# An expert layer whose row loads go four per unit, and a late row fetch that moves to one queue

## The chip, the cores and the metric

The kernel runs on one core of a Trainium2 chip. Its engines are TensorE (PE, matrix products; PEld is its weight load), VectorE (DVE), ScalarE (ACT), GpSimd (POOL) and SyncE (SP, which issues transfers). The metric is the device time in microseconds of one execution, lower is better.

## The reference, cut to what matters

```python
x = attention(q, k, v)                       # 4608 tokens of 512, linear attention with decay
logits = x @ w_gate                          # 8 experts
expert_idx = argmax(logits, axis=1)
gate_w = softmax(logits)[arange(N), expert_idx]
for e in range(8):                           # each token goes to one expert
    mask = expert_idx == e
    h = maximum(x[mask] @ w1[e], 0.0)        # 512 -> 1024
    out[mask] = gate_w[mask, None] * (h @ w2[e])   # 1024 -> 512
h = maximum(out @ w_in, 0.0)                 # the dense layer, 512 -> 2048
return (h * h) @ w_out                       # 2048 -> 512
```

## The kernel before

The kernel has three parts, and each begins before the one ahead of it has ended. The first, to about 185 us, computes attention and leaves the tokens as rows in DRAM (`x_d`) with their logits (`l_d`), and sorts the tokens by expert: `qidx` and `gidx` hold, for each expert, up to 640 rows in five tiles of 128.

The second is the expert layer, about 185 to 750 us. It is a loop over 64 units `u`, eight for each expert `e` (`f` is the unit within it). A unit holds 128 of the 1024 hidden features. In TensorE's order iteration `u` computes the first product of unit `u + 1` (`first`, lines 806 to 808, 24 matmuls on two halves of 320 tokens) and the second product of unit `u` (`second`, lines 830 to 832, 15 matmuls). Every product is split in a high and a low part, so there are three matmuls where one would do. Between the two products ScalarE takes the positive part of a half into `hh` (line 812) and VectorE the remainder into `hl` (line 813). The buffer of `hh` and `hl` has six places; the second product of the last six units is done at the end.

While expert `e` runs, the rows of expert `e + 1` are fetched. In the iteration with `f == 0`, `gather(e + 1)` puts 20 indirect loads on POOL's queue (line 270, tile `xs`: five tiles of 128 rows, each in four quarters of 512 bytes a row), and with `f == 1` five loads of the logits of those rows follow (tile `glg`). An indirect load is an instruction of POOL, and POOL takes its instructions in order. Two units after its own number (three for the rows of expert 1) a tile is turned by VectorE (`transp`, line 778). When an expert's last unit is done, `finish` scales its five accumulators on ScalarE (line 841) and POOL writes them to their rows of `y_d` (line 291). These writes stand ahead of the next expert's loads on POOL. The gate of an expert is computed at its unit 5 from the logits that came in.

Beside this SyncE loads the experts' weights (line 107), and VectorE and ScalarE prepare the weights of the dense layer, a job in nearly each unit.

The third part is the dense layer, in five steps of row tiles. It needs rows of `y_d` of all experts. While the last expert's five tiles are finished one after the other, SyncE fetches the first row tiles (`fetch`, line 709, four parts each, tile `yi`), VectorE turns them (line 722), sums and splits them (lines 734 and 747), and the first products of the dense layer (line 1146) follow. A fetch of rows waits for the writes of `y_d` issued so far. The tile numbered 3 is fetched in the last turn of that loop; behind it SyncE issues two loads of weight tiles (`stream`, line 319, 1 MB each).

Of the kernel before, what the change touches and what calls it, by code (L numbers as in the profile page):

```python
# [7 lines left out]
F32 = mybir.dt.float32  # L8
# [5 lines left out]
ALU = mybir.AluOpType  # L14
# [8 lines left out]
CT = CAP // 128  # L23
# [4 lines left out]
LEAD = 2  # L28
# [21 lines left out]
def body(ctx, tc, att, tab_v, tab_x, masks, wg, ident, pick, cst, wu, wd, out):  # L50
    nc = tc.nc
    vec, act, pe, pool, sp = nc.vector, nc.scalar, nc.tensor, nc.gpsimd, nc.sync

    def scope(stack, name, bufs, space=None, side=None, reuse=None):
        kw = {"space": space, "side": side, "reuse_waits": reuse}
        kw = {k: v for k, v in kw.items() if v is not None}
        return stack.enter_context(tc.tile_pool(name=name, bufs=bufs, **kw))

    const = scope(ctx, "const", 1)
    xs_p = scope(ctx, "xs_p", 1)  # L60
# [11 lines left out]
    x_d = dram.tile([NTOK, 512], F32, name="x_d")  # L72
# [10 lines left out]
    gidx = places.tile([128, NS], I32, name="gidx")  # L83
# [10 lines left out]
    qidx = places.tile([128, 4, NS], I32, name="qidx")  # L94
# [10 lines left out]
    def load_unit(u, on=None):  # L105
        raw = on.tile([128, CT, 4, 128], F32, tag="xs", name="raw").rearrange("p a b c -> p (a b c)")[:, 0:1024] if on else pools["stg"].tile([128, 1024], F32, tag="raw", name="raw")
        sp.dma_start(out=raw, in_=wu[u])
        return raw
# [18 lines left out]
    def load_wide(v, s):  # L127
        raw = pools["cr_p"].tile([128, 512, 2], I32, tag="craw", name="craw")
        sp.dma_start(
            out=raw.rearrange("p n t -> p (n t)"), in_=wd[v, :, 512 * s:512 * s + 512].bitcast(I32)  # L130
        )
        return raw
# [124 lines left out]
    def indices(rt, n, inv, gi, si, gf=None):  # L257
        f = rt.tile([128, n], F32, tag="f", name="f")
        vec.scalar_tensor_tensor(
            out=f, in0=inv[:, n:2 * n], scalar=128.0, in1=inv[:, 0:n], op0=ALU.mult, op1=ALU.add  # L260
        )
        for o in (gi, gf):
            if o is not None:
                vec.tensor_scalar(out=o, in0=f, scalar1=-1.0, scalar2=0.0, op0=ALU.add, op1=ALU.max)
        g = rt.tile([128, n], F32, tag="g", name="g")
        vec.tensor_scalar(out=g, in0=inv[:, 0:n], scalar1=0.0, scalar2=FAR, op0=ALU.is_equal, op1=ALU.mult)
        vec.scalar_tensor_tensor(out=si, in0=f, scalar=-1.0, in1=g, op0=ALU.add, op1=ALU.add)

    def fetch_rows(xs, src, index):
        pool.indirect_dma_start(  # L270
            out=xs, out_offset=None, in_=src, in_offset=bass.IndirectOffsetOnAxis(ap=index, axis=0),
        )
# [8 lines left out]
    x_q = x_d.rearrange("n (a c) -> (n a) c", a=4)  # L281
# [46 lines left out]
    with ExitStack() as es:  # L328
# [307 lines left out]
        for t in range(NT):  # L636
# [3 lines left out]
            if t in (1, 2, 4):  # L640
                c = {1: 2, 2: 3, 4: 4}[t]
# [53 lines left out]
    yi = {}  # L695

    def columns():
        return [xt_p.tile([128, 4, CAP], F32R, tag=f"xt{s}", name=f"xt{s}") for s in range(2)]


    def rows_of(t):

        return y_d[128 * t:128 * t + 128, :].rearrange("(t i) (a c) -> a i t c", i=32, a=4)
# [3 lines left out]
    def fetch(dst, t, known=True, on=None, parts=range(4)):  # L707
        for a in parts:
            d = (on or sp).dma_start(out=dst[32 * a:32 * a + 32], in_=rows_of(t)[a])
            if not known:  # L710
                for p in sent:
                    tc.add_manual_dep(
                        d.ins, p.name,
                        mybir.DependencyInfo(mybir.DependencyClass.Sync, mybir.DependencyReason.DATA),
                        reason="the rows come from all of them",
                    )
                if len(yi) < 2:
                    read.append(d.ins)
# [32 lines left out]
    with ExitStack() as es:  # L751
# [3 lines left out]
        acc_a = scope(es, "acc_a", 1, PSUM, reuse="tile")  # L755
        xs_t, xt_t, lg_t, h_t, acc, gate = {}, {}, {}, {}, {}, {}

        def gather(e):
            xt_t[e] = columns()
            xs = xs_p.tile([128, CT, 4, 128], F32, tag="xs", name="xs")  # L760
            for i in range(0 if e else LEAD, CT):
                j = CT * e + i
                if e == 0:
                    fetch_rows(xs[:, i].rearrange("p q c -> p (q c)"), x_d[:, :], gidx[:, j:j + 1])
                    continue
                for q in range(4):
                    fetch_rows(xs[:, i, q], x_q, qidx[:, q, j:j + 1])
            xs_t[e] = xs

        def transp(e, i):  # L770
            xs = xs_t[e]
# [158 lines left out]
        tiles = range(LEAD)  # L930
# [18 lines left out]
        ends.pop(0)()  # L949
        steps[4]()  # L950
        indices(rt, NS, inv, gidx, sidx, gidf)
        gather(0)
        for f in ends:
            f()
        top = rt.tile([128, 1], F32, tag="top", name="top")
# [17 lines left out]
        sm = scope(es, "sm", 2, reuse="tile")  # L973
# [37 lines left out]
        for u in range(NU):  # L1011
            e, f = divmod(u, 8)
            v = u + AHEAD + 1
            if v < NU:
                raw[v] = load_unit(v)
            if u + 1 in work:
                what, j, r = work[u + 1]
                if what != "sum":
                    wide.append(load_wide(2 * j + r, 0 if what == "in" else 1))
            v = u + AHEAD  # L1020
            job, rests = None, []
            if last_job:
                f_ = next(last_job)
                if f_:
                    f_()
                last_job = None
            if v in raw:
                rests.append(split_unit(v, raw.pop(v), vec))
            if u in work:
                what, j, r = work[u]  # L1030
                if what == "in":
                    job = narrow(wide.pop(0), ("ca", "cb")[r], made)
                elif what == "sum":
                    job = left_factors(j, *made[2 * j:], r)
                else:
                    job = split_wide(2 * j + r, wide.pop(0))
            if v == NU + 2:
                assert not last_job and not wide
                early.close()
                w_d = scope(late_es, "w_d", 4, side="right", reuse="tile")  # L1040
                x0_p = scope(late_es, "x0_p", 1, side="right", reuse="tile")
            if v in (NU, NU + 1):
                stream(w_a, 4 + v - NU)
            if v >= NU + 2:
                stream(w_d, v - NU - 2)
            if e + 1 < NE:
                if f == 0:
                    gather(e + 1)
                if f == 1:
                    lg_t[e + 1] = fetch_logits(sm, gidx[:, CT * (e + 1):CT * (e + 2)], CT)  # L1050
            if e + 1 < NE:
                turns = {3: [0], 4: [1], 5: [2], 6: [3, 4]} if e == 0 else {i + 2: [i] for i in range(CT)}
                rests += [transp(e + 1, i) for i in turns.get(f, [])]
            for f_ in rests[:1]:
                f_()
            if job:
                next(job)
            for f_ in rests[1:]:
                f_()
            if u == NU - 3:  # L1060
                with tc.block():
                    tc.mark_branch_hint_location("rest", "LikelyTaken", [mybir.EngineType.PE])
            if u + 1 < NU:
                first(u + 1, (1,) if u + 1 < MORE else (0, 1))
            if f == 5:
                gate[e] = gate_of(sm, lg_t.pop(e), CT)
            if job:
                next(job)
                last_job = job
            if u < NU - FIN:  # L1070
                second(u, range(LEAD if u < MORE else 0, CT))
                if f == 7:
                    finish(e)
        rest_of()
        for i in range(CT):
            for u in range(NU - FIN, NU):
                second(u, [i])
            if i == CT - 1:
                turn(yi[0][:, 3], x0_t[0][:, 1], None)
                low = first_row(1, 4, 2)  # L1080
                fetch(yi[0][:, 2], 3, False, sp, (0, 1))
                fetch(yi[0][:, 2], 3, False, pool, (2, 3))
                for f in low:
                    f()
                for _ in range(2):
                    stream(w_a)
            finish(NE - 1, [i])
            if i < 2:
                if i == 0:
                    yi[0] = xs_p.tile([128, CT, 4, 128], F32, tag="xs", name="yi")  # L1090
                fetch(yi[0][:, 2 + i], i, False)
            if i == 2:
                fetch(yi[0][:, 4], 2, False)
            if i == 3:
                first_factors()
                turn(yi[0][:, 2], x0_t[0][:, 0], None)
                for f in first_row(0, 4, 2):
                    f()
# [383 lines left out]
```

## Time and profile before

| what | value |
|---|---|
| runs | 1487.53, 1497.63, 1511.9 us; median 1497.63 |
| profiled execution | 1501.78 us, its span 1500.0 us |
| TensorE busy | 1387.7 us, 93% of the span |
| VectorE, ScalarE, POOL busy | 832.5, 547.7, 357.4 us |
| mean granted clock of TensorE | 0.954 |

Busy time of an engine is the time in which its instructions ran; matmuls are pipelined, so a busy TensorE is not one at its peak. [...] In the rows below a bracket gives the idle time of the engine just before the instruction, and what ended it; "issue" means that the profile shows nothing that was waited for, "remote" that the signal's origin was not found.

### The profile page before, as it was taken

The numbers are of one execution on the slowest core, as the hardware profiler recorded it, in microseconds if no ns is written. First come the engines' busy times: TensorE is split into PE (matmuls) and PEld (weight loads), VectorE is DVE, ScalarE is ACT, GpSimd is POOL, SyncE is SP. The second block draws the span as 40 slices with busy tenths as digits, with TensorE's granted clock in tenths as the row PEclk, the third lists the DMA queues.
The fourth block names the chain that finished last, engine by engine and source line by source line (L and its number), as shares of the span: only waits on it lengthen the run. The fifth ranks groups of instructions, "written<-read, shape, count | busy, mean of one in ns | idle before, by whom it ended". The sixth has DMA issues, their size and how long they took to land. (4 is left out here: it accounts for less than half of the span.)

```text
span 1500.0 us, 21528 instructions
## 1 busy us (share of the span) xinstructions
PE 1387.7 (93%) x8121; PEld 1174.6 (78%) x8121; DVE 832.5 (56%) x1512; ACT 547.7 (37%) x1064; POOL 357.4 (24%) x368
## 2 busy tenths in 40 slices
PE   8989998596959897989989999999999999999998
PEld 6877797394939685969888888888888888888887
DVE  5767766383838584866368646524563456435422
ACT  1222333251515252434245444424442344334421
POOL 2232275425160716261122101200030002100000
PEclk9999998696969997989999999999999999999999
DMA  9999745262636554554768566665666566665563
GB/s 317 317 281 290 217 156 170 84 225 86 234 97 208 187 190 153 191 168 165 258 215 299 206 212 231 226 222 201 220 225 222 208 218 234 217 217 196 196 225 113
DMA packets 107488, 311.02 MB, mean 207 GB/s; under 512 B 20430, under 2 KB 55502, under 8 KB 85360
## 3 DMA queue, kind: packets, MB, share of 16 engines
q1 hardware_dynamic: 97440, 288.28, 56.4%
q0 software_dynamic: 9936, 21.28, 4.7%
q8 instruction: 66, 1.08, 0.3%
q14 instruction: 46, 0.38, 0.1%
HBM read 257.98 MB, written 52.58 MB: 207 GB/s over the span
## 5 line engine op out<-in xcount | busy, mean ns | idle before, releaser
L1146 PE MATMUL b<-xt,wq 128*128 128x512 f32 (+1 forms) x1296 | 266.8, 364 | 6.3 <-ACT xt L743 5.3
L1146 PEld LDWEIGHTS b<-xt,wq 128*128 128x128 f32 x1296 | 222.8, 190 | 45.4 <-ACT xt L743 5.9
L1218 PE MATMUL fa<-wq,ch 128*128 128x512 f32 x576 | 224.1, 389 | 0.0
L1219 PE MATMUL fa<-wq,ch 128*128 128x512 f32 x576 | 224.1, 389 | 0.0
L1220 PE MATMUL fa<-wq,cl 128*128 128x512 f32 x576 | 224.1, 389 | 0.0
L1208 DVE TENSOR_TENSOR cl<-g,ch 128x512 fp32r<-128x512 f32 (+1 forms) x160 | 108.8, 688 | 174.4 <-ACT ch L1207 171.9
L734 POOL TENSOR_TENSOR xsum<-yf 128x256 f32<-128x256 f32 x80 | 63.7, 804 | 455.5 <-DVE yf L722 392.0
L807 PE MATMUL l<-xt,w 128*128 128x320 f32 (+1 forms) x480 | 153.7, 320 | 19.1 <-issue 19.0
L808 PE MATMUL l<-xt,w 128*128 128x320 f32 (+1 forms) x480 | 154.1, 321 | 17.3 <-issue 17.3
L806 PE MATMUL l<-xt,w 128*128 128x320 f32 (+1 forms) x480 | 152.8, 318 | 17.7 <-issue 17.3
L270 POOL DMA_INDIRECT xs<-x_d,qidx x140 | 148.2, 1058 | 44.2 <-issue 41.2
L1207 ACT ACTIVATE ch<-g 128x512 fp32r<-128x512 f32 (+1 forms) x160 | 91.5, 584 | 183.5 <-PE fa L1219 183.5
L813 DVE SCALAR_TENSOR_TENSOR hl<-l,hh 128x320 fp32r<-128x320 f32 (+2 forms) x128 | 59.2, 484 | 171.3 <-ACT hh L812 102.8
L812 ACT ACTIVATE hh<-l 128x320 fp32r<-128x320 f32 (+2 forms) x128 | 55.0, 436 | 271.3 <-remote 136.7
L830 PE MATMUL acc<-w,hh 128*128 128x512 f32 x320 | 132.5, 414 | 10.8 <-issue 10.2
L831 PE MATMUL acc<-w,hh 128*128 128x512 f32 x320 | 131.4, 411 | 6.7 <-issue 6.6
L832 PE MATMUL acc<-w,hl 128*128 128x512 f32 x320 | 130.8, 409 | 7.2 <-issue 6.8
L1220 PEld LDWEIGHTS fa<-wq,cl 128*128 128x128 f32 x576 | 108.1, 188 | 22.6 <-DVE cl L1208 0.2
L1219 PEld LDWEIGHTS fa<-wq,ch 128*128 128x128 f32 x576 | 108.1, 188 | 22.5
L1218 PEld LDWEIGHTS fa<-wq,ch 128*128 128x128 f32 x576 | 108.1, 188 | 22.3
L807 PEld LDWEIGHTS l<-xt,w 128*128 128x128 f32 x480 | 93.1, 194 | 25.1 <-issue 22.9
L808 PEld LDWEIGHTS l<-xt,w 128*128 128x128 f32 x480 | 93.4, 195 | 22.7 <-issue 22.7
(182 smaller groups left out, 2084.0 us busy)
## 6 DMA issues: line engine op xcount, KB each, us to landing
wq<-ws_d SPq DMA_DIRECT2D x142, 1024.0 KB
raw<-wu SPq DMA_DIRECT2D x62, 512.0 KB
in<-att SPq DMA_DIRECT2D x28, 1024.0 KB
craw<-wd SPq DMA_DIRECT2D x32, 512.0 KB
ws_d<-cw SPq DMA_DIRECT2D x24, 512.0 KB
x_d<-xr SPq DMA_DIRECT2D x144, 64.0 KB
out<-fo SPq DMA_DIRECT2D x32, 256.0 KB
yq<-y_d SPq DMA_DIRECT2D x112, 64.0 KB
```

Source lines behind the costliest of these rows:

```text
L270: pool.indirect_dma_start(out=xs, out_offset=None, in_=src, in_offset=bass.IndirectOffsetOnAxis(ap=index, axis=0),)
L806: pe.matmul(ps, w[:, 0, k], hi[:, k, cs], start=(k == 0), stop=False)
L807: pe.matmul(ps, w[:, 0, k], lo[:, k, cs], start=False, stop=False)
L808: pe.matmul(ps, w[:, 1, k], hi[:, k, cs], start=False, stop=(k == 3))
L830: pe.matmul(acc[i], hh[:, cs], w[:, 0], start=(f == 0), stop=False)
L831: pe.matmul(acc[i], hh[:, cs], w[:, 1], start=False, stop=False)
L832: pe.matmul(acc[i], hl[:, cs], w[:, 0], start=False, stop=(f == 7))
L1146: pe.matmul(ps, w[:, a, c], xc[T][i, b][c], start=(i in (5, 1, 4) and m == 0), stop=(m == 5), skip_group_check=True,)
L1208: vec.tensor_tensor(out=lo[:, o], in0=s, in1=hi[:, o].bitcast(F32), op=ALU.subtract)
L1218: pe.matmul(acc[i], hi[:, cs], w[:, 0], start=(f == 0), stop=False)
L1219: pe.matmul(acc[i], hi[:, cs], w[:, 1], start=False, stop=False)
L1220: pe.matmul(acc[i], lo[:, cs], w[:, 0], start=False, stop=(f == 15))
```

## The change

In the expert layer `gather(e + 1)` is called in the iterations with `f` from 0 to 4, for one row tile (four loads) each, and the logits are fetched with `f == 5`. Ahead of each of these, POOL gets a small instruction, the tick: it adds one element of `hh` of unit `u` to itself, into a tile that nobody reads. POOL can go on when ScalarE has written the first half of that unit's `hh`; for the first six units, whose first 256 tokens are computed apart, that element is written before the loop. In the last turn of the loop over the last expert's tiles, all four parts of row tile 3 are fetched by SyncE, where before two were SyncE's and two POOL's.

```diff
-        def gather(e):
-            xt_t[e] = columns()
-            xs = xs_p.tile([128, CT, 4, 128], F32, tag="xs", name="xs")
-            for i in range(0 if e else LEAD, CT):
+        def gather(e, tiles):
+            if e not in xs_t:
+                xt_t[e] = columns()
+                xs_t[e] = xs_p.tile([128, CT, 4, 128], F32, tag="xs", name="xs")
+            for i in tiles:
                 j = CT * e + i
...
                 for q in range(4):
-                    fetch_rows(xs[:, i, q], x_q, qidx[:, q, j:j + 1])
-            xs_t[e] = xs
+                    fetch_rows(xs_t[e][:, i, q], x_q, qidx[:, q, j:j + 1])
...
             if e + 1 < NE:
-                if f == 0:
-                    gather(e + 1)
-                if f == 1:
+                if f <= CT:
+                    tick = sm.tile([1, 1], F32, tag="tick", name="tick")
+                    here = h_t[u][0][0:1, 0:1].bitcast(F32)
+                    pool.tensor_tensor(out=tick, in0=here, in1=here, op=ALU.add)
+                if f < CT:
+                    gather(e + 1, [f])
+                if f == CT:
                     lg_t[e + 1] = fetch_logits(sm, gidx[:, CT * (e + 1):CT * (e + 2)], CT)
...
-                fetch(yi[0][:, 2], 3, False, sp, (0, 1))
-                fetch(yi[0][:, 2], 3, False, pool, (2, 3))
+                fetch(yi[0][:, 2], 3, False)
```

On POOL, while an expert runs, between the writes of the finished rows (`y_d`) and the next ones stand the row loads (`xs`) and the logit loads (`glg`); the lines with - are before's, those with + the changed kernel's, and a line without a sign is in both:

```order
 L291 DMA y_d<-y,sidx 4608x512 x5
-L270 DMA xs<-x_d,qidx 128x128 x20
+L1050 TENSOR_TENSOR tick<-hh 1x1
+L270 DMA xs<-x_d,qidx 128x128 x4
+L1050 TENSOR_TENSOR tick<-hh 1x1
+L270 DMA xs<-x_d,qidx 128x128 x4
+L1050 TENSOR_TENSOR tick<-hh 1x1
+L270 DMA xs<-x_d,qidx 128x128 x4
+L1050 TENSOR_TENSOR tick<-hh 1x1
+L270 DMA xs<-x_d,qidx 128x128 x4
+L1050 TENSOR_TENSOR tick<-hh 1x1
+L270 DMA xs<-x_d,qidx 128x128 x4
```

One run of 20 loads has become five runs of four with a tick ahead of each; a sixth tick stands ahead of the five logit loads, which keep their place behind the rows.

On POOL, at the end of the expert layer, stand the last expert's five writes of `y_d` and the fetches of rows (`yi`, then `yq` for the next step of the dense layer):

```order
-L291 DMA y_d<-y,sidx 4608x512 x4
-L709 DMA yi<-y_d 32x4x128 x2
-L291 DMA y_d<-y,sidx 4608x512
+L291 DMA y_d<-y,sidx 4608x512 x5
 L709 DMA yq<-y_d 32x4x128 x16
```

On SyncE, at the same place, the row fetches (`yi`) and the weight tiles behind them (`wq`):

```order
-L709 DMA yi<-y_d 32x4x128 x14
+L709 DMA yi<-y_d 32x4x128 x16
 L319 DMA wq<-ws_d 128x2048 x12
```

The two fetches have left POOL, where they stood ahead of the last write, and stand on SyncE ahead of the weight tiles.

## Rows read from the trace of the kernel before

**Rows 1.** The page's head: span and instructions.
```profile
span 1500.0 us, 21528 instructions
```

**Rows 2.** Three windows: each engine's busy time (count), granted clock, DMA share.
```profile
core 0: us, PE busy (x) PEld busy (x) DVE busy (x) ACT busy (x) POOL busy (x), PEclk, DMA share, GB/s
186.00:199.00 13.00, 12.89 (x83) 11.53 (x82) 8.10 (x17) 5.24 (x10) 9.17 (x9) 1.00 0.29 76
346.00:370.00 24.00, 9.79 (x23) 5.59 (x23) 0.91 (x3) 1.17 (x3) 14.56 (x16) 0.59 0.22 58
377.00:404.00 27.00, 27.00 (x155) 24.68 (x154) 22.81 (x43) 12.28 (x23) 0.00 (x0) 1.00 0.67 224
```

**Rows 3.** Windows over seven slow stretches, 228:241 to 657:671: their sum.
```profile
sum 147.00, PE 71.55 PEld 45.12 DVE 37.55 ACT 24.35 POOL 85.34; mean PE 10.22 PEld 6.45 DVE 5.36 ACT 3.48 POOL 12.19
```

**Rows 4.** Timeline of TensorE in one of them: start, duration (us), line, operation.
```profile
353.69 0.59 PE L831 MATMUL acc<-w,hh 128*128 128x512 f32 x1 [0.81 <-issue]
```

**Rows 5.** Timeline of POOL: first writes per expert; first row and last logit load.
```profile
247.00 1.18 POOL L291 DMA_INDIRECT y_d<-y,sidx  x1 [13.48 <-ACT y L841]
...
326.19 1.16 POOL L291 DMA_INDIRECT y_d<-y,sidx  x1 [40.06 <-ACT y L841]
...
333.31 0.99 POOL L270 DMA_INDIRECT xs<-x_d,qidx  x1 [0.30 <-issue]
...
364.19 0.95 POOL L270 DMA_INDIRECT glg<-l_d,gidx  x1 [0.30 <-issue]
...
404.51 1.24 POOL L291 DMA_INDIRECT y_d<-y,sidx  x1 [39.38 <-ACT y L841]
...
483.34 1.01 POOL L291 DMA_INDIRECT y_d<-y,sidx  x1 [40.14 <-ACT y L841]
...
553.27 1.31 POOL L291 DMA_INDIRECT y_d<-y,sidx  x1 [28.84 <-ACT y L841]
...
625.02 1.19 POOL L291 DMA_INDIRECT y_d<-y,sidx  x1 [31.13 <-ACT y L841]
...
694.45 1.01 POOL L291 DMA_INDIRECT y_d<-y,sidx  x1 [27.38 <-ACT y L841]
```

**Rows 6.** Timeline of ScalarE, line 812: activations of some halves, in order of time.
```profile
289.91 0.77 ACT L812 ACTIVATE hh<-l 128x320 fp32r<-128x320 f32 x2 [16.30 <-remote]
...
366.38 0.44 ACT L812 ACTIVATE hh<-l 128x320 fp32r<-128x320 f32 x1 [21.32 <-remote]
...
379.54 0.44 ACT L812 ACTIVATE hh<-l 128x320 fp32r<-128x320 f32 x1 [2.03 <-PE l L808]
...
400.36 0.44 ACT L812 ACTIVATE hh<-l 128x320 fp32r<-128x320 f32 x1 [3.24 <-PE l L808]
...
447.40 0.77 ACT L812 ACTIVATE hh<-l 128x320 fp32r<-128x320 f32 x2 [20.54 <-remote]
...
517.09 0.44 ACT L812 ACTIVATE hh<-l 128x320 fp32r<-128x320 f32 x1 [6.43 <-PE acc L832]
...
596.71 0.77 ACT L812 ACTIVATE hh<-l 128x320 fp32r<-128x320 f32 x2 [14.10 <-remote]
...
655.93 0.44 ACT L812 ACTIVATE hh<-l 128x320 fp32r<-128x320 f32 x1 [4.30 <-PE acc L832]
```

**Rows 7.** Timeline from 748 us: SyncE's and POOL's issues, VectorE, TensorE.
```profile
748.41 0.78 SPq L709 DMA_DIRECT2D yi<-y_d  x2
...
749.28 0.85 SPq L319 DMA_DIRECT2D wq<-ws_d  x2
...
749.60 1.22 POOL L709 DMA_DIRECT2D yi<-y_d  x2 [3.10 <-DVE xt L747]
...
752.27 0.42 DVE L747 TENSOR_TENSOR xt<-xsum,xt 128x256 fp32r<-128x256 f32 x1
757.36 0.71 DVE L722 STREAM_TRANSPOSE x<-yi 128x512 f32<-128x512 f32 x1 [4.67 <-DMA yi<-y_d]
...
758.57 1.68 PE L1146 MATMUL b<-xt,wq 128*128 128x256 f32 x5 [4.58 <-ACT xt L743]
```

More of the change, by code (lines that the diff above doesn't have):

```diff
@@ L756, in body @@
         xs_t, xt_t, lg_t, h_t, acc, gate = {}, {}, {}, {}, {}, {}
-        def gather(e):
-            xt_t[e] = columns()
-            xs = xs_p.tile([128, CT, 4, 128], F32, tag="xs", name="xs")
-            for i in range(0 if e else LEAD, CT):
+        def gather(e, tiles):
[3 more added lines that the diff above has]
+            for i in tiles:
                 j = CT * e + i
                 if e == 0:
-                    fetch_rows(xs[:, i].rearrange("p q c -> p (q c)"), x_d[:, :], gidx[:, j:j + 1])
+                    fetch_rows(xs_t[e][:, i].rearrange("p q c -> p (q c)"), x_d[:, :], gidx[:, j:j + 1])
                     continue
                 for q in range(4):
-                    fetch_rows(xs[:, i, q], x_q, qidx[:, q, j:j + 1])
-            xs_t[e] = xs
+                    fetch_rows(xs_t[e][:, i, q], x_q, qidx[:, q, j:j + 1])
         def transp(e, i):
@@ L951, in body @@
         indices(rt, NS, inv, gidx, sidx, gidf)
-        gather(0)
+        gather(0, range(LEAD, CT))
         for f in ends:
```

## The prediction

> **What bounds the kernel now.** The span is 1500.0 us [rows 1], and TensorE is the engine on the path for almost all of it, so I looked for the stretches in which it does little. I read the busy time by 10 us windows between 185 and 840 us first, then the waits of TensorE, then the timelines of GpSimd (POOL) and ScalarE (ACT). In this text stage e is the stretch in which expert e's eight units are computed; while it runs, the rows of expert e+1 are fetched.
>
> The windows show two kinds of stretch [rows 2]. From 377 to 404 us TensorE is busy throughout at a granted clock of 1.00 and does 155 matmuls in 27 us, 5.7 a microsecond. From 346 to 370 us it does 23 in 24 us, about one a microsecond, at a granted clock of 0.59, while POOL is busy and VectorE, ScalarE and the DMA engines have little to do. There are seven such stretches, one in every stage from 0 to 6, together 147 us in which POOL is busy 85 us and TensorE 72 us [rows 3]. TensorE's own rows there wait for nothing the profile can name: "issue" [rows 4].
>
> The POOL timeline tells what they have in common [rows 5]. In stage 2 POOL writes expert 1's finished rows from 326.19, then issues 20 row loads and 5 logit loads back to back, from 333.31 to 364.19: 30.9 us for 24 intervals, 1.29 us each. The slow stretch begins in the middle of this burst and ends about 5 us after its last load. ScalarE shows the same from the other side: the activation of unit 3's first half stands at 366.38 after 21.32 us of idle time [rows 6], although TensorE was busy with the next work from 346 on. It reads like a signal from TensorE that comes late and a queue behind it that fills. I know no cause from the rows; I know that every such stretch lies under the second half of a long burst, and that a short one does no harm: from 186 to 199 us POOL issues eight loads and an elementwise operation, and TensorE is busy for 12.89 of 13.00 us at clock 1.00 [rows 2].
>
> **What it costs now.** A unit at full rate takes (400.36 - 379.54) / 3 = 6.94 us [rows 6], so eight take 55.5 us. The first writes of finished rows of experts 0 and 6 lie 694.45 - 247.00 = 447.5 us apart [rows 5]; six stages at full rate would be 333.1. So stages 1 to 6 lose 114 us, 19 each.
>
> **Change 1, loads in groups of four.** The 140 row loads and 35 logit loads remain, in the same order. Added are 6 ticks in each of seven stages, 42 in all, each reading one element of the current unit's activations. The trace has no such operation; I bound it by nothing and by the 1.29 us of a whole load, 7.7 us a stage. It lies on POOL, which stands idle 13 to 40 us before a stage's first write of finished rows [rows 5]; that cover is wide enough, and I take it at nothing. What counts is the wait that a tick carries: behind it on POOL stand the rest of the loads and then the writes of finished rows.
>
> Which ticks wait? Unit k of a stage lets group k go; the logits go with unit 5. POOL reaches the first group 7.1 us after the first write of finished rows (333.31 - 326.19), and a group takes 4 x 1.29 = 5.1 us. A unit takes 6.94 us, so as long as TensorE runs at full rate POOL, which starts late, finds each tick's activation there already. Groups 0, 1 and 2 therefore still form one run of 12 loads behind the five writes, and TensorE slows as before. But then the activations are late, and the ticks bite:
> - Stage 1: first write 247.00, plus 7.1 and 15.4: groups 0 to 2 done at 269.6; unit 3's activation comes at 289.91. Held: groups 3 and 4 and the logits, 13 loads. Stage 2 likewise, with 348.8 against 366.38, and stage 3, with 427 against 447.40: 13 each.
> - Stage 4: four groups done at 511; unit 4 comes at 517.09, so group 4 goes soon after. I count the logits alone: 5. Stage 6 likewise (652.7 against 655.93): 5.
> - Stage 5: four groups done at 581; unit 4 at 596.71: 9.
> The activation times are [rows 6], the first writes [rows 5]. Together 58 loads in 13 groups, 58 x 1.29 = 75 us by which the long bursts end earlier and TensorE comes back earlier.
>
> In stage 0 nothing is held. There a tick reads the first column of an activation tile, which for units 0 to 5 is written from the two leading tiles before the loop begins. Its slow stretch, 228 to 241 us, stays.
>
> The held groups come later, one by one, each behind its own unit. What does one of them cost TensorE? Bounds: nothing, as in the stretch from 186 to 199 [rows 2]; or a slow spell of its own, as long as the group (5.1 us) and a tail of 5 us, in which TensorE does 0.96 matmuls a microsecond in place of 5.74 and so loses 10.1 x 0.83 = 8.4 us. A held group is half as long as the harmless burst, so I take a value near the low end, 1.5 us, for the cases in which two groups follow closely: 13 x 1.5 = 20 us. Net 75 - 20 = 55 us.
>
> Late rows cost nothing: tile i is turned two units after its group is let go, 13.9 us, of which the group takes 5.1; 8.8 us are left for the landing, and the slowest load from POOL that I found, beside two weight tiles, took 757.36 - 749.60 = 7.8 us [rows 7]. VectorE is the next bound: 22.81 of 27.00 us busy at full rate [rows 2]. It holds.
>
> **Change 2, the last late rows.** Between the expert layer and the dense one VectorE waits 4.67 us, to 757.36, for rows whose second half POOL asked for at 749.60, after SyncE had asked for two weight tiles at 749.28; TensorE stands still for 4.58 us, to 758.57 [rows 7]. In the new order SyncE issues all four parts ahead of the tiles; its first two go at 748.41 and take 0.78 us to issue, so the other two go by about 750.0. If the rows land at once, VectorE, free at 752.69, starts 4.67 us earlier and the whole 4.58 us are gained; if they land as late as now, nothing is. I take 4 us. The weight tiles are asked for 0.8 us later, which the trace hides: no TensorE row in this stretch waits for them.
> [...]
>
> **Sum.** 1501.8 (the profiled execution's own time, 4 us above the median of the runs) - 55 - 4 = **1443 us**.
>
> **The rivals.**
> - *No slow stretch is left.* If the bursts must be unbroken and a tick breaks them enough, all 114 us go: 1501.8 - 114 - 4 = 1384. For it: nothing harmful is seen in the short burst [rows 2]. Against it: at full rate the first three groups follow each other without a pause.
> - *The loads are not what slows TensorE, or the ticks come too late.* The slow stretches stay, only change 2 counts: 1498. For it: 12 loads and 5 writes still run unbroken, the ticks of stage 0 hold nothing, and no row names POOL as what TensorE waits for. Against it: seven stretches of seven end with the burst. [...]
> - *Slower: every group let go starts a new slow spell.* The price is the upper bound, 8.4 us for each of 13 held groups, 109 us, against 75 saved: 1501.8 - 75 + 109 - 4 = 1532. It decides the sign from 75 / 13 = 5.8 us a group. For it: after a pause TensorE restarts at the lower clock (0.59 on average in the stretch). Against it: 186 to 199 us.
>
> **How the numbers follow.** The forecast has 0.50, no stretch left 0.20, no effect 0.20, slower 0.10. The forecast's own range takes 0 to 4 us for a held group: 1423 to 1475. The range for all reaches from the first rival, 1384, to just above the second, 1500; what lies beyond are the slower case and the edges, 0.2 together. A measurement of this kernel can tell about 2% from no change, 30 us. Faster by more: nearly all of the forecast and the first rival, 0.67; within 2%: the second rival and the forecast's upper edge, 0.22; slower: 0.11.
>
> **What would show it.** In the profile of the changed kernel: ticks of stages 1 to 6 that wait for ScalarE before group 3 or 4; slow stretches of about 8 us in place of 24 in stage 2 and 3; the stage length, first write to first write, at 62 to 70 us in place of 70 to 79; the stage 0 stretch unchanged; VectorE's turn of the late rows right behind the work ahead of it, and no gap of TensorE there. I am wrong if the ticks never wait, if TensorE still stands at one matmul a microsecond while POOL waits, or if each group has a stretch of its own.

## The result and the profile after

| | before | after |
|---|---|---|
| median of the runs (range, number) | 1504.95 us (1487.53 to 1513.13, 6) | 1410.79 us (1394.46 to 1419.49, 6) |
| ratio, with its 95% interval | | 0.9365 (0.9319 to 0.9411) |
| profiled execution, its span | 1501.78, 1500.0 us | 1416.54, 1414.7 us |
| first writes of experts 0 and 6, apart | 447.5 us [rows 5] | 365.2 us |

The kernel is faster by 94 us in the medians. That is within the range for all (1384 to 1500) and below the forecast's own range (1423 to 1475); the forecast was 1443. The ratio is of the fast runs alone, without the two slowest of the changed kernel, of which the profiled execution is one. The head of the page after, as [rows 1]:

```profile
span 1414.7 us, 21636 instructions
...
PE 1359.7 (96%) x8121; PEld 1161.9 (82%) x8121; DVE 831.8 (59%) x1512; ACT 547.0 (39%) x1064; POOL 375.4 (27%) x408
```

The windows of after: the stretch of stage 0, then of stage 2 the first part of the burst and the 24 us of [rows 2] that were slow before (columns as there).

```profile
core 0: us, PE busy (x) PEld busy (x) DVE busy (x) ACT busy (x) POOL busy (x), PEclk, DMA share, GB/s
228.00:241.00 13.00, 9.37 (x40) 6.64 (x39) 3.20 (x10) 2.07 (x4) 7.22 (x9) 0.85 0.19 59
319.00:346.00 27.00, 26.02 (x146) 23.31 (x145) 17.58 (x29) 9.06 (x15) 21.94 (x23) 1.00 0.68 218
346.00:370.00 24.00, 23.47 (x129) 20.80 (x128) 20.92 (x40) 11.25 (x22) 5.01 (x6) 1.00 0.53 178
```

From 346 to 370 us TensorE does 129 matmuls where it did 23, at a granted clock of 1.00, full speed, where it had 0.59. Of stage 2's burst, which now runs from 317.40 to 354 us, these 24 us hold only the end; the first of the two windows covers most of it, with 146 matmuls in 27 us. Stage 0 still has its slow stretch. The timeline of POOL, as [rows 5]: first writes, and in stage 2 two groups of loads with the tick between them, then the last tick.

```profile
250.63 1.18 POOL L291 DMA_INDIRECT y_d<-y,sidx  x1 [13.43 <-ACT y L841]
...
310.16 1.32 POOL L291 DMA_INDIRECT y_d<-y,sidx  x1 [15.35 <-ACT y L841]
...
322.19 0.94 POOL L270 DMA_INDIRECT xs<-x_d,qidx  x1 [0.30 <-issue]
323.14 0.18 POOL L1050 TENSOR_TENSOR tick<-hh 1x1 f32<-1x1 f32 x1
323.47 1.48 POOL L270 DMA_INDIRECT xs<-x_d,qidx  x1
...
347.72 0.18 POOL L1050 TENSOR_TENSOR tick<-hh 1x1 f32<-1x1 f32 x1 [1.86 <-ACT hh L812]
...
370.75 1.22 POOL L291 DMA_INDIRECT y_d<-y,sidx  x1 [16.34 <-ACT y L841]
...
615.86 1.01 POOL L291 DMA_INDIRECT y_d<-y,sidx  x1 [16.40 <-ACT y L841]
```

Stage 1 takes 59.5 us where it took 79.2, stage 2 60.6 where it took 78.3. But the tick at 323.14 waits for nothing: the next load starts 1.28 us after the last, where two loads without a tick between them lie 1.25 apart. Over the whole run the ticks wait little; the view of the tick's tile:

```profile
L1050 POOL TENSOR_TENSOR tick<-hh x42: 182/183/1009, 200.6 to 592.2; 1x1 f32<-1x1 f32 x42
its engine sat idle before it (us, times) until:
  ACT hh L812: 9.6, 6
```

Six ticks of 42 wait for ScalarE, 9.6 us in all. The forecast's chain went through 75 us of held loads; so the gain is there, and its reason as forecast is not.

The end of the expert layer, as [rows 7]: SyncE's issues, VectorE's turn of the late rows, TensorE.

```profile
661.75 9.96 SPq L709 DMA_DIRECT2D yi<-y_d  x12
...
670.55 13.79 PE L1149 MATMUL b<-xt,wq 128*128 128x256 f32 x108 [0.67 <-ACT xt L743]
...
671.80 0.85 SPq L319 DMA_DIRECT2D wq<-ws_d  x2
...
674.00 0.70 DVE L722 STREAM_TRANSPOSE x<-yi 128x512 f32<-128x512 f32 x1
```

VectorE no longer waits, and TensorE does its first 108 products of the dense layer without a gap.

### The profile page after: what moved, and what is told of

Its sections match the earlier page's. It is cut to its first block, busy times and chain, and to the rows that moved or that the text cites. A ratio compares the mean times of both kernels' runs of the same rounds, so it can differ in the third digit from the quotient of the medians.

```text
span 1414.7 us, 21636 instructions
## 1 busy us (share of the span) xinstructions
PE 1359.7 (96%) x8121; PEld 1161.9 (82%) x8121; DVE 831.8 (59%) x1512; ACT 547.0 (39%) x1064; POOL 375.4 (27%) x408
## 4 chain that ended last, share of the span: by engine, by line
PE 77%; DMA 10%; issue 6%; POOL 2%; DVE 2%; ACT 1%; another core or an unknown queue 1%; SPq 1%; POOLq 0%; DVEq 0%; ACTq 0%
PE b L1149 23%; PE fa L1223 9%; PE fa L1221 9%; PE fa L1222 9%; DMA in<-att 5%; PE l L808 4%; PE acc L830 4%; PE l L807 4%; PE l L806 4%; PE acc L831 4%; PE acc L832 4%; DMA raw<-wu 1%; POOL xs L270 1%; DMA x_d<-xr 1%
## 5 line engine op out<-in xcount | busy, mean ns | idle before, releaser
L270 POOL DMA_INDIRECT xs<-x_d,qidx x140 | 154.9, 1106 | 40.0 <-issue 34.9
L806 PE MATMUL l<-xt,w 128*128 128x320 f32 (+1 forms) x480 | 150.5, 314 | 6.7 <-issue 5.0
L808 PE MATMUL l<-xt,w 128*128 128x320 f32 (+1 forms) x480 | 150.6, 314 | 5.1 <-issue 5.0
L807 PE MATMUL l<-xt,w 128*128 128x320 f32 (+1 forms) x480 | 150.7, 314 | 4.3 <-issue 4.2
L831 PE MATMUL acc<-w,hh 128*128 128x512 f32 x320 | 128.5, 402 | 3.0 <-issue 3.0
L830 PE MATMUL acc<-w,hh 128*128 128x512 f32 x320 | 129.1, 403 | 2.2 <-issue 1.8
L832 PE MATMUL acc<-w,hl 128*128 128x512 f32 x320 | 127.9, 400 | 2.4 <-issue 2.4
L1135 ACT ACTIVATE s<-b 128x512 f32<-128x512 f32 (+1 forms) x120 | 66.5, 555 | 104.8 <-PE b L1149 104.6
L813 DVE SCALAR_TENSOR_TENSOR hl<-l,hh 128x320 fp32r<-128x320 f32 (+2 forms) x128 | 59.3, 485 | 79.7 <-ACT hh L812 54.0
L806 PEld LDWEIGHTS l<-xt,w 128*128 128x128 f32 x480 | 90.9, 189 | 9.5 <-issue 4.8
```

The lines of the kernel that those rows point to most:

```text
L270: pool.indirect_dma_start(out=xs, out_offset=None, in_=src, in_offset=bass.IndirectOffsetOnAxis(ap=index, axis=0),)
L806: pe.matmul(ps, w[:, 0, k], hi[:, k, cs], start=(k == 0), stop=False)
L807: pe.matmul(ps, w[:, 0, k], lo[:, k, cs], start=False, stop=False)
L808: pe.matmul(ps, w[:, 1, k], hi[:, k, cs], start=False, stop=(k == 3))
L830: pe.matmul(acc[i], hh[:, cs], w[:, 0], start=(f == 0), stop=False)
L831: pe.matmul(acc[i], hh[:, cs], w[:, 1], start=False, stop=False)
```

## The experiments

Two theories stood at the start. W: a tick helps by what it holds back. B: a tick helps because it stands between loads, even if it does not wait. A third, R, came from the first results: what counts is how closely the loads follow each other. In all tables a stage is measured from first write to first write on POOL's timeline; at full rate it takes 55.5 us, six take 333.1. The runs fell on four chips, named A to D; the chip of the first runs of before and after is not recorded.

**Ticks that cannot wait, and a tick ahead of every load** (chip A, where before took 1500.43 us).

```diff
 free ticks:
-                    here = h_t[u][0][0:1, 0:1].bitcast(F32)
+                    here = idn[0:1, 0:1]             # a constant
 a tick ahead of every load (25 a stage; constant, or this unit's hh):
                 for q in range(4):
+                    beat()
                     fetch_rows(xs_t[e][:, i, q], x_q, qidx[:, q, j:j + 1])
```

> The changed kernel, but each of the 42 ticks reads a constant that was there before the loop, so no tick can wait; the groups of four, the order and change 2 are as in the changed kernel. Theory W (the wait counts: what a tick holds back is what helps): the loads go back to back as before, all that is left is change 2: about 1500 us. Theory B (the break counts: any elementwise operation of POOL between loads ends what a burst builds up): as the changed kernel, about 1411 us, within 10 us.

> A tick that never waits (it reads a constant) ahead of every single row load and logit load of stages 0 to 6, in place of one ahead of each group of four; change 2 kept. [...] Theory W: as free ticks, about 1500 us.

> A tick that reads the current unit's activations ahead of every single load. Theory B: the same as with the ticks that never wait ahead of every load, 1370 to 1390 us. Theory W: ticks wait no longer than in the changed kernel, since a unit's later ticks find the activation there: about 1411 us, the changed kernel's time.

| | median, us | ratio to before (95%) | stages 1 to 6, us | sum | mean pace of the 25 loads, us |
|---|---|---|---|---|---|
| before | 1500.43 | | 79.2 78.3 78.8 69.9 71.8 69.4 | 447.5 | 1.29 to 1.42 |
| free ticks | 1438.27 | 0.9591 (0.9541 to 0.9641) | 70.0 61.8 64.3 61.9 69.5 59.5 | 387.0 | 1.37 to 1.47 |
| after | 1410.79 | 0.9365 (0.9319 to 0.9411) | 59.5 60.6 61.7 60.9 61.0 61.5 | 365.2 | 1.44 to 1.55 |
| every load, free | 1382.52 | 0.9195 (0.9149 to 0.9241) | 57.8 60.3 59.3 59.7 56.0 55.0 | 348.0 | 1.49 to 1.65 |
| every load, waiting | 1380.11 | 0.9210 (0.9170 to 0.9250) | 56.6 59.0 53.8 57.5 56.6 53.3 | 336.9 | 1.56 to 1.68 |

(The stages of before and after are those of the first profiles; the time and ratio of after are of the first runs too, not of chip A.) All these kernels but before have change 2. Neither theory gave 1438. With ticks that wait for nothing the kernel is 62 us faster than before, and stages 1 to 6 are 60.5 us shorter, so W falls as the main cause. With waiting ticks these stages are another 21.8 us shorter, and on chip A the kernel with waiting ticks takes 1414.26 us even without change 2 (next experiment), 24 less than free ticks; so B as first put falls too. With a tick ahead of every load it no longer matters whether it waits. Here are the windows of the same 60 us in free ticks, in every load free, and in every load waiting:

```profile
250.00:310.00 60.00, 52.77 (x252) 45.38 (x252) 35.72 (x65) 22.41 (x39) 33.26 (x36) 0.88 0.51 171
```
```profile
250.00:310.00 60.00, 58.77 (x325) 52.71 (x324) 47.70 (x85) 27.81 (x47) 42.54 (x58) 1.00 0.63 211
```
```profile
250.00:310.00 60.00, 59.65 (x338) 54.34 (x337) 48.59 (x86) 28.18 (x49) 44.17 (x60) 1.00 0.63 212
```

252, 325 and 338 matmuls: the closer the loads, the fewer. That is theory R. What a tick puts between two loads can be read from POOL's timeline: the gap between the end of a row load and the start of the next is 0.30 us without a tick (133 gaps in before), 0.48 in the mean with a free tick (28 gaps), 0.70 with the waiting ticks of after (28), 0.50 and 0.52 with a tick ahead of every load (133 each). Over the 20 row loads of a stage free ticks so add 4 x 0.18 = 0.7 us, after 1.6, a tick ahead of every load 19 x 0.2 = 3.8; what a stage loses goes from 19.1 us over 9.0 and 5.3 to 2.5 and 0.6. After has no more ticks than free ticks have, only their waits, so it is the distance and not the number of ticks that separates these two. Between before and free ticks both differ, the distance and the ticks as such. Stage 0 speaks for the distance: there the six ticks of after wait for nothing, the loads' pace is 1.41 us as against 1.40 in before, and from first load to first write it takes 48.2 us as against 48.0.

**Change 2 left out** (chip A).

```diff
-                fetch(yi[0][:, 2], 3, False)
+                fetch(yi[0][:, 2], 3, False, sp, (0, 1))
+                fetch(yi[0][:, 2], 3, False, pool, (2, 3))
```

> The changed kernel without change 2 (the last late rows are again asked for half by SyncE, half by POOL, POOL's half behind the two weight tiles). My prediction's term for change 2 is 4 us (bounds 0 and 4.6): 1415 us. [...]

The median is 1414.26 us (1407.53 to 1418.05), ratio 0.941 (0.9363 to 0.9457): the interval overlaps that of after, so the medians don't settle a few us. The trace does. TensorE's timeline, and its windows:

```profile
664.24 4.84 PE L1150 MATMUL b<-xt,wq 128*128 128x256 f32 x36 [0.67 <-ACT xt L743]
674.22 11.58 PE L1150 MATMUL b<-xt,wq 128*128 128x256 f32 x72 [5.14 <-ACT xt L743]
```
```profile
669.00:674.20 5.20, 0.08 (x1) 0.00 (x0) 1.14 (x2) 0.42 (x1) 0.50 (x1) 0.92 0.69 224
674.20:679.00 4.80, 4.78 (x21) 4.61 (x22) 3.94 (x7) 2.51 (x6) 0.74 (x2) 0.50 0.07 27
```

The gap of 5.14 us is back, and behind it TensorE runs at clock 0.50 for about 5 us, 21 matmuls where after does 41 from 675 to 680 us. The first 108 products take 21.56 us (664.24 to 685.80) against 13.79: change 2 is worth 7.8 us against this run. By the same reckoning before took 20.4 us (749.14 to 769.56), so 6.6. The short idle time ahead of the first of these products, 0.67 or 0.68 us, is the same in all three kernels.

**Four ticks in a row, and the rows by other ways** (chip B).

```diff
 four in a row (on the changed kernel, so with change 2):
+                    for _ in range(4 if f < CT else 5):   # 25 a stage, as above
+                        tick = sm.tile([1, 1], F32, tag="tick", name="tick")
+                        pool.tensor_tensor(out=tick, in0=idn[0:1, 0:1], in1=idn[0:1, 0:1], op=ALU.add)
 whole rows (on the kernel before; the way of expert 0's rows, for all experts):
+                    fetch_rows(xs[:, i].rearrange("p q c -> p (q c)"), x_d[:, :], gidx[:, j:j + 1])
 plain transfers (on the kernel before; r a multiple of 128), from sp or from pool:
+                    sp.dma_start(out=xs[:, i, q], in_=x_q[r:r + 128])
```

> As many non-waiting ticks per stage as in the run with one ahead of every load (25), but standing together: four ahead of each group of four row loads, five ahead of the logit loads. Theory B (a break ends what builds up; one break is as good as four in a row): as with one non-waiting tick per group, about 1438 us. Theory R (the rate counts: loads closer than some 1.5 us on average pile work up, whatever stands between them): the mean interval goes from 1.43 to about 1.55 us, so about as with a tick ahead of every load, 1382 to 1400 us.

> The kernel before, with one edit: each row tile of experts 1 to 7 is fetched by one load of whole rows (128 rows of 2 KB) in place of four of quarter rows (512 B), as expert 0's are. 10 loads instead of 25 in a burst, the same bytes, no tick, no change 2. Theory N (the number of loads, or of descriptors, piles up): a burst of 10 ends before TensorE suffers, as the eight loads from 186 to 199 us; nearly all of 114 us goes: 1385 to 1400 us. Theory V (the bytes that the loads move are what TensorE waits behind): the bytes come 2.5 times as fast, the slow stretch starts earlier and stays about as long: 1490 to 1510 us.

> The kernel before, with the rows of experts 1 to 7 fetched by 140 plain transfers from SyncE in place of POOL's indirect loads; they fetch 128 neighbouring rows and not the routed ones, so that part of the computation is changed. POOL keeps the five writes and the five logit loads of a stage. Theory P (POOL's indirect loads slow TensorE): the seven slow stretches are gone and about 114 us with them, 1385 to 1395 us. Rival (the landing of 20 x 64 KB among the weight tiles is what disturbs TensorE): the stretches stay, about 1500 us.

> The kernel before, with the rows of experts 1 to 7 fetched by 140 plain (not indirect) transfers of POOL; they fetch 128 neighbouring rows and not the routed ones, so that part of the computation is changed. Before, POOL's plain transfers of the dense part took 0.55 to 0.62 us against 1.06 for an indirect load. Theory P1 (any transfer that POOL issues piles up): 20 in a row at half the interval, TensorE slow as before, about 1480 to 1500 us. Theory P2 (only the indirect kind does): as with SyncE's, 1385 to 1395 us.

All four took the time of before on that chip, and before itself took 1378.56 us there (31 runs, 1374.16 to 1383.97), 8% less than on chip A: 1378.88, 1377.10, 1381.01 and 1380.10 us, ratios 0.9993 (0.9972 to 1.0013), 1.0002, 1.0014 and 1.0011. They tell nothing on the theories, since there was nothing to repair, but something larger: **on this chip before does not lose the time of the slow stretch**, and its mean granted clock is 0.990 to 0.999, where on chip A it is 0.948 to 0.957. Without any row load of POOL (SyncE's transfers) it takes no less. Change 2 is worth nearly as much here as on chip A, and only the first of the four kernels has it. TensorE's first 108 products of the dense layer, with four ticks in a row and then with whole rows:

```profile
634.51 13.78 PE L1149 MATMUL b<-xt,wq 128*128 128x256 f32 x108 [0.67 <-ACT xt L743]
```
```profile
622.68 4.85 PE L1146 MATMUL b<-xt,wq 128*128 128x256 f32 x36 [0.68 <-ACT xt L743]
631.75 10.54 PE L1146 MATMUL b<-xt,wq 128*128 128x256 f32 x72 [4.22 <-ACT xt L743]
```

That is 13.78 us against 19.61, and 19.97 and 20.14 in the other two kernels without change 2. A kernel that has these 6 us and takes the time of before spends them elsewhere: by an estimate from these numbers, 25 ticks a stage in groups cost some 6 us here, and the interval of the ratio is about 3 us either way. No profile of before was kept on this chip, so where they go is open.

**All ways in one kernel.** So that a single execution tells apart what it can on whichever chip it gets, the next kernels fetch in another way in each stage.

> One kernel, another way of fetching in each stage (each stage fetches for the next expert), to be read stage by stage, from a stage's first write of finished rows to the next; change 2 kept. Stage 0: as before (20 row loads and 5 logit loads back to back); 1: whole rows, 5 loads of 2 KB rows instead of 20 of 512 B; 2: 20 plain POOL transfers; 3: four non-waiting ticks ahead of each group of four; 4: as before; 5: 20 plain SyncE transfers; 6: as before. Whole rows and plain transfers bring other rows or another order of columns, so that part of the computation is changed. Unhindered a stage takes 55.5 us. Theory R (a POOL indirect load every 1.3 us piles work up, one every 1.55 us nearly not): stages 1 (10 loads only), 2 and 5 55 to 57 us, stage 3 57 to 60, stage 4 and, by its windows, stage 6 70 to 79. Theory B (one break or four in a row is the same): stage 3 62 to 70. Theory V (the bytes): stage 1 70 to 79. If any POOL transfer does it: stage 2 70 to 79. On a chip where the kernel before takes 1378 us instead of 1500 none of this shows: all stages 54 to 58, those as before too.

> The same with the ways in other stages, so that place and way come apart. Stage 0: as before; 1: four non-waiting ticks ahead of each group of four; 2: plain SyncE transfers; 3: as before; 4: whole rows; 5: plain POOL transfers; 6: a non-waiting tick ahead of every load. Whole rows and plain transfers bring other rows or another order of columns, so that part of the computation is changed. Theory R: stage 1 57 to 60 us, 2, 4 and 5 55 to 57, 3 70 to 79. Theory B: stage 1 62 to 70. Theory V: stage 4 70 to 79. If any POOL transfer does it: stage 5 70 to 79. On a chip where the kernel before takes 1378 us all stages 54 to 58.

Both keep change 2 and fell on chip C (before 1382.43 us, one run; these 1376.84 and 1377.13, one run each): stages of 54.3 to 56.9 us, of every kind. The 5 to 6 us between them and before are what change 2 is worth. The windows of the first over stage 0, and over the burst and what follows it in stage 4, both loading as before:

```profile
202.00:241.00 39.00, 39.00 (x215) 35.77 (x214) 27.00 (x44) 17.84 (x29) 27.38 (x25) 1.00 0.56 185
416.00:430.00 14.00, 14.00 (x80) 12.78 (x79) 12.77 (x23) 5.70 (x11) 11.06 (x10) 1.00 0.73 241
430.00:452.00 22.00, 22.00 (x125) 20.02 (x124) 16.20 (x31) 10.42 (x18) 16.24 (x15) 1.00 0.71 238
```

25 loads back to back, and TensorE is busy throughout. In the second kernel stage 3 loads as before too, at a pace of 1.42 us, where stage 3 of before has 1.29, although nothing was put between the loads. (In stages 0 and 4 the paces are nearly alike: 1.41 and 1.40 here, 1.40 and 1.38 in before.) A row load is longer beside a busy VectorE: in before 0.95 us in the mean where VectorE was busy for under a tenth of the load (54 loads), 1.14 where it was busy for over half of it (74). So the pace is partly a consequence of the slowness: where TensorE falls behind, VectorE has less to do (0.91 of 24 us from 346 to 370 us [rows 2]), and POOL's loads come faster still. That can be why so little distance does so much, and it means that only runs which set the distance from outside, as the ticks do, speak on the cause.

**The same on chip D** (before 1506.67 us, 11 runs), with the changed kernel beside it.

> One kernel, another way of fetching in each stage, to be read stage by stage. Stage 0: as before; 1: four non-waiting ticks ahead of each group of four; 2: whole rows, 10 loads in all; 3: plain POOL transfers; 4: as stage 1; 5: as before; 6: plain SyncE transfers. Whole rows and plain transfers bring other rows or another order of columns, so that part of the computation is changed. On a chip where the kernel before takes about 1500 us: theory R (rate) stages 1 and 4 57 to 60 us, 2 and 3 55 to 57, 5 70 to 79; theory B (one break or four in a row is the same) stages 1 and 4 62 to 70; theory V (bytes) stage 2 70 to 79; if any POOL transfer does it, stage 3 70 to 79. On a chip where the kernel before takes about 1380 us: all 54 to 58.

> The changed kernel itself, once more, on the chip that this call gets. Two of the three chips on which the kernel before is timed with the experiments so far gave 1378 and 1382 us for it, one 1500. Theory C (the slow stretch is the chip's, and the change only repairs it): where before takes about 1380 us the changed kernel takes the same within 1%, 1370 to 1385 us, all of it change 2's 4 us at most; where before takes about 1500, 1411 us. Rival (the groups of four help anywhere): some per cent faster on either.

Here the slow stretch exists, and the stages come apart. POOL's first writes in the mixed kernel, most of the plain transfers of stage 3 between them, and the windows over the bursts of stages 0 to 5, with two for stage 5:

```profile
245.74 1.19 POOL L293 DMA_INDIRECT y_d<-y,sidx  x1 [15.97 <-ACT y L860]
...
300.09 1.01 POOL L293 DMA_INDIRECT y_d<-y,sidx  x1 [7.99 <-ACT y L860]
...
356.57 1.22 POOL L293 DMA_INDIRECT y_d<-y,sidx  x1 [35.82 <-ACT y L860]
...
368.07 6.84 POOL L783 DMA_DIRECT2D xs<-x_d  x13 [0.18 <-issue]
...
411.38 1.02 POOL L293 DMA_INDIRECT y_d<-y,sidx  x1 [29.96 <-ACT y L860]
...
468.59 1.22 POOL L293 DMA_INDIRECT y_d<-y,sidx  x1 [8.85 <-ACT y L860]
...
543.39 1.20 POOL L293 DMA_INDIRECT y_d<-y,sidx  x1 [34.45 <-ACT y L860]
```
```profile
220.00:240.00 20.00, 15.46 (x58) 11.17 (x56) 8.78 (x19) 5.00 (x10) 7.60 (x8) 0.74 0.27 92
253.00:292.00 39.00, 39.00 (x225) 35.79 (x224) 30.07 (x55) 15.34 (x28) 32.02 (x46) 1.00 0.62 210
307.00:321.00 14.00, 14.00 (x80) 12.77 (x79) 10.86 (x18) 3.66 (x6) 10.70 (x11) 1.00 0.85 297
363.00:382.00 19.00, 19.00 (x111) 17.50 (x110) 16.65 (x29) 7.24 (x13) 15.65 (x25) 1.00 0.80 266
419.00:460.00 41.00, 41.00 (x233) 37.46 (x232) 32.05 (x58) 17.90 (x33) 33.68 (x46) 1.00 0.66 222
475.00:490.00 15.00, 14.96 (x84) 13.32 (x82) 11.34 (x19) 5.25 (x8) 11.65 (x12) 1.00 0.75 263
490.00:518.00 28.00, 13.85 (x44) 9.78 (x44) 8.82 (x15) 5.94 (x10) 14.68 (x15) 0.63 0.38 124
```

- Four ticks in a row, stages 1 and 4: 54.3 and 57.2 us, TensorE busy throughout. The same six breaks, one tick each, gave 59.5 to 70.0 on chip A, and with the waits of the changed kernel 59.2 to 63.6 on this one. B falls, R stands: the gap at a break was 1.27 us in place of 0.48, the pace 1.57 and 1.62 us.
- Whole rows, stage 2: 56.5 us. The same bytes in 5 loads instead of 20 do no harm, so theory V, the bytes, falls.
- Plain transfers of POOL, stage 3: 54.8 us, although 13 of them went in 6.84 us, 0.53 each. Not any transfer of POOL does it: the indirect kind, 25 in a row, does.
- As before, stage 5: 74.8 us. In its first 15 us, 84 matmuls; in the 28 us after, 44 at clock 0.63. Stage 0 has the same at 220 to 240 us. The burst does harm only from its middle on, as in [rows 2].
- Plain transfers of SyncE, stage 6: 58.5 us (to 601.85), where 55 to 57 stood in the first mixed kernel's expectation. TensorE waited 2.3 us for VectorE there. The same transfers took 58.3 us in stage 6 on chip B too, with 2.1 us of such waits, so this is not the slow stretch; why TensorE waits there was not followed up.

Each way but "as before" and the four ticks stands in one stage of one execution here. The changed kernel took 1406.99 us on this chip, ratio 0.9333 (0.9281 to 0.9385), stages of 59.2 to 63.6 us: as the first time. What it takes on chip B or C was not measured; the four kernels of chip B and the two of chip C speak for no gain there beyond the 6 us of change 2, less what the ticks cost.

The pace against the loss, over the 45 stages with 25 loads that were profiled on chips A and D and in the first two runs:

| mean pace, us | stages | us above 55.5 (range) |
|---|---|---|
| 1.29 to 1.31 | 3 | 23.3 (22.8 to 23.7) |
| 1.35 to 1.40 | 5 | 15.7 (14.0 to 19.3) |
| 1.40 to 1.45 | 7 | 8.0 (6.2 to 13.9) |
| 1.45 to 1.55 | 13 | 4.2 (-0.1 to 6.0) |
| 1.55 to 1.68 | 17 | 2.6 (-2.2 to 8.1) |

The highest values of the last row, 8.1 and 7.8 us, are of the changed kernel: waits ahead of the last rows and of the logits (3.81 and 1.45 us, 2.99 and 2.25) raise the mean pace, but the groups ahead of them are as close as ever. The mean is not all; evenly spread ticks do better at the same mean (a waiting tick ahead of every load, at 1.56 to 1.68 us: -2.2 to 3.5).

The prediction reads the 21.32 us of [rows 6] as a signal from TensorE that comes late. In before the last matmul of that half on record ends at 343.55 us, and its activation starts at 366.38. What lies between, a queue or anything else, is not shown: on the chips with the slow stretch records of these signals are missing (last section), and what is left of them can't be matched with the instructions.

## Why the prediction was right, and where it was not

The direction was right for the reason given at the outset: the loads' bursts are where TensorE loses time, and breaking them up helps. The size was worked out through waits that did not occur, and the result missed the forecast's own range. That it lies in the range for all is owed to that range's width, from one rival to the other; so far it is luck.

- **What bounds it.** Right in place: the seven slow stretches were the loss, and they go with the loads' burst. Right too that the burst must be long. Not foreseen: that this holds on some chips only.
- **"Groups 0, 1 and 2 therefore still form one run of 12 loads behind the five writes, and TensorE slows as before."** This is the step that failed. Six ticks that wait for nothing already shorten stages 1 to 6 by 60.5 us of the 114 lost. In the changed kernel a stage loses 5.3 us and not 19.1, and little bites: 6 waits and 9.6 us, where I had 58 loads and 75 us held. The step "I take it at nothing" is the same error from the other side: I priced the tick as work on POOL and not as distance between loads, and 0.7 us of distance in a burst of 30 was worth half of the loss.
- **The sum.** Stages 1 to 6 gave 82.2 us (447.5 to 365.2) and not 55, out of the 114 there were; 32 are still lost, 5.3 a stage. Change 2 gave 6.6 and not 4: the gap of 4.58 us is gone as forecast, and I had left out the 2.0 us that TensorE then loses at clock 0.50 (20.4 - 4.58 - 13.8). The first write of expert 0 came 3.6 us later. 82.2 + 6.6 - 3.6 = 85.2, the difference of the two profiled executions (1501.78 - 1416.54 = 85.24).
- **What would show it.** Stage 0 unchanged: yes here (first load to first write 48.2 us against 48.0), no in the second profile of the changed kernel (40.1), where the loads went at 1.50 us instead of 1.41. Stage length 62 to 70: it is 59.5 to 61.7. "I am wrong if the ticks never wait" came nearly true.
- **The rivals.** "No slow stretch is left", with its condition that "a tick breaks them enough", was nearer in mechanism than the forecast; its 1384 us is what a tick ahead of every load reaches. "The loads are not what slows TensorE" fell with whole rows and plain transfers on chip D. No run shows at which place TensorE is held up; they show only that it slows under POOL's indirect loads on some chips (44 matmuls in 28 us at clock 0.63 in stage 5 on chip D), and that POOL's plain transfers (111 in 19 us at clock 1.00 in stage 3) and loads with four ticks between groups (225 in 39 us at clock 1.00 in stage 1) left it busy throughout. The slower case fell: it counted 8.4 us for each held group, and a whole stage of the changed kernel loses 5.3.
- **What was in the trace of before already.** The loads of stages 1 to 3 go at 1.29 to 1.31 us and lose 23 us, those of stages 4 to 6 at 1.36 to 1.42 and lose 14 to 16. I read one mean, 1.29, and counted held loads; the slope between the two halves would have suggested that some hundredths of a microsecond of pace go with several of loss, though not which of the two brings about the other.

A version that beats both kernels is a tick ahead of every load (1380 us on chip A, where before takes 1500; by the ratios 1.7% below the changed kernel, with intervals that don't touch). The 1.7% compares ratios of different chips. Where there is no slow stretch it was not run; 25 ticks a stage in groups of four took the time of before on chip B (1378.88 against 1378.56) together with change 2, so they may cost what change 2 gives there, some 6 us.

## What to carry to other kernels

Where an engine falls behind during a burst that it doesn't wait for, look at the pace of the burst before counting what could be held back: set the pace (a cheap instruction between the items, fewer and larger items, another kind of transfer), and see the loss follow. Compare like stages of one trace with each other; their differences are experiments that have been run already. And repeat the kernel before on more than one chip before calling a stall the kernel's: one execution with another variant in each stage tells on any chip which of the two it is.

## What the runs showed of the hardware

- **Chips differ.** The kernel before took 1500.43 and 1506.67 us on chips A and D and 1378.56 and 1382.43 on B and C, with no slow stretch on C at the same burst. Each chip's executions were made at one time, so whether it is the chip or the occasion is not shown.
- **On the chips with the slow stretch, records of semaphores are missing from the trace, in before only beside indirect transfers.** There, from 375 to 400 us (no POOL transfer), 67 instructions of the four engines raise their semaphore and 67 changes are recorded, and from 450 to 475 (none either) 65 and 65; from 325 to 350 (18 indirect transfers) 59 and 31. On chip C, from 425 to 450 (18 indirect transfers), 59 and 59. But on chips A and D they are missing as well where TensorE is not slowed: with a waiting tick ahead of every load on chip A, from 260 to 285 us, 70 and 39, while TensorE was busy for 25.00 of 25.00 us at clock 1.00; with whole rows on chip D, from 300 to 320 us, 57 and 21, while it was busy for 20.00 of 20.00. So missing records alone do not mean a slow TensorE. Whether the recording also holds TensorE up, so that the slow stretch is partly made by it, is **open**: every execution timed here comes with a granted clock, so none shows the kernel without any recording.
- **Whether the number of indirect loads or of the row pieces that they fetch counts** is open as well: whole rows cut both by four (5 loads of 128 rows in place of 20 of 128 quarter rows).
- **A gap of 5 us costs more than itself.** Behind it TensorE's clock was 0.50 for about 5 us, where the same products ran at 1.00 without the gap. Beyond the gap itself 2.0 us were lost in before, 2.6 with change 2 left out on chip A, and 1.6 to 1.7 in the three kernels without change 2 on chip B.
